# Loading the first 240 tokens of q and k as plain fp32 on two hardware queues, with a new load order, in an attention-plus-MLP kernel

## The chip, the cores and the metric

The kernel runs on one core of one Trainium2 chip. The time is the device time of one execution in microseconds (us). A ratio in this document is the record's comparison of one kernel's fast runs with the fast runs of the kernel before on the same chip; it differs by up to 0.001 from the plain quotient of the two means, and is not the ratio of the medians quoted beside it. A run counts as slow, and is set aside, when it is over 1.5% above the fastest of its kernel; the runs set aside here had a clock of 0.986 to 1.0, so a late load could have made them long as well. Chips differ: the kernel before had a median of 350.9 us on one, 352.4 to 352.9 us on three occasions later.

Words used for the engines: PE is TensorE (PEld its weight loads), DVE is VectorE, ACT is ScalarE, POOL is GpSimd, SP is SyncE. In this kernel each engine runs its instructions in the order in which they were emitted (the 7.82 us wait below shows it for PE). A DMA queue takes its transfers from one engine's order too: q1 is SyncE's queue, q10 is ScalarE's, both fed by hardware; q0 is GpSimd's queue, fed by software, and the only one here whose transfers also convert fp32 to bf16. The profile counts all of them against the same 16 DMA engines.

## The reference, cut to what matters

```python
# q, k, v: [8, 8, 576, 64] fp32; beacon_k, beacon_v: [8, 8, 16, 64] fp32
k_all = concatenate([beacon_k, k], axis=2)            # 592 keys, the first 16 always visible
v_all = concatenate([beacon_v, v], axis=2)
scores = (1 / 8) * q @ k_all^T                        # causal mask on the 576 own keys
a = softmax(scores)
x = (a @ v_all) as [8 * 576, 512]
out = relu(x @ w_in) ** 2 @ w_out                     # 512 -> 2048 -> 512
```

## The kernel before

A list scheduler written in Python orders all operations at build time, with estimated durations. Each engine then executes its fixed list. Batch 0 is split into two parts (its first 240 tokens, then 336) so that the tensor engine can start early; batches 0 and 1 are transposed on the tensor engine, later batches by transposing DMAs. The parts that the change touches:

```python
def add_part_loads(b, part, prio, after, free):      # q/k of batches 0 and 1: GpSimd's queue, cast on the way
    ...
    return [nc.gpsimd.dma_start(out=strided_buf(b, x, part)[:, h],               # bf16
            in_=t[b, h, t0:t0 + np_ * ns, :].rearrange("h (p s) d -> p h s d", s=ns))]

def add_load(b, x, c, prio, behind=[], sync=[]):      # one chunk of 128 rows as fp32, to be cast by an engine
    soft = b in SOFT_V or (b == 0 and c >= 2)         # V chunks 2 to 4 of batch 0: GpSimd's queue
    queue = nc.gpsimd if soft else nc.sync            # V chunks 0 and 1: SyncE's queue
    ...                                               # [128, 8, 64] fp32: pieces of 256 bytes
    engs = ("POOL", "DVE") if b == 0 else ("POOL",)   # who casts it

def add_beacon(b, prio):                              # 32 KB for each of batches 0 and 1
    nc.sync.dma_start(out=bkf[b % 2], in_=beacon_k[b]...)     # bkf is ONE buffer; SyncE's queue
    # DVE casts it, PE transposes it (4 small matmuls), DVE copies it into kT

# order of the first loads on GpSimd's queue:
#   part 0 of q/k, w_in quarter 0, part 1 of q/k, V chunks 2 to 4, w_in quarters 1 to 3, batch 1's q/k, ...
# order of the first loads on SyncE's queue:
#   beacon k 0, beacon v 0, V chunks 0 and 1, beacon k 1, then (after the last w_out load) batch 2 ...
```

The softmax here doesn't subtract the row's maximum and nothing guards it: scores larger than these inputs give would overflow.

## Time and profile before

| | before |
|---|---|
| time, median | 350.9 us |
| span of the profiled run | 348.6 us |
| PE busy | 330.0 us |
| PE idle in the first 15 us | 8.8 us |
| first scores | 9.43 us |
| first AV | 11.32 us |
| transposes of part 1 begin | 14.88 us |

The first fence has lines of the page of the kernel before: the busy time of PE, then the busy tenths of PE and of the DMA engines in 40 equal slices of the span.

```profile
PE 330.0 (95%) x2846; PEld 175.8 (50%) x2884; DVE 171.1 (49%) x394; ACT 191.7 (55%) x290; POOL 92.2 (26%) x139
...
PE   1899999999989979999999999999999999999995
...
DMA  9999979999999999899996999560015011011002
```

PE is the limit nearly everywhere, and the DMA engines are about as busy in the first two thirds. The windows view of the kernel before gives, for each stretch of time, its length, then the busy us and the number of instructions of each engine, the granted clock, the DMA engines' busy share and the GB/s.

```profile
0.00:5.00 5.00, 0.25 (x4) 0.25 (x4) 3.01 (x19) 1.49 (x2) 3.75 (x9) 1.00 0.50 83
5.00:10.00 5.00, 1.71 (x20) 1.00 (x20) 1.75 (x6) 0.66 (x3) 4.99 (x11) 1.00 1.32 162
10.00:15.00 5.00, 4.22 (x52) 2.62 (x54) 4.03 (x17) 3.75 (x7) 4.72 (x6) 1.00 1.44 190
15.00:20.00 5.00, 5.00 (x66) 3.02 (x66) 3.95 (x14) 3.34 (x7) 3.45 (x6) 1.00 1.21 228
20.00:25.00 5.00, 5.00 (x60) 3.42 (x57) 3.07 (x11) 3.50 (x7) 1.95 (x3) 1.00 1.24 207
25.00:30.00 5.00, 5.00 (x75) 3.41 (x73) 4.04 (x16) 4.68 (x9) 1.79 (x2) 1.00 1.30 204
```

The first number behind the comma is PE. In the first 15 us it works 6.18 us and idles 8.82; from then until 60 us it idles only 0.1 us. Those 8.8 us are what the change goes for. The timeline of the kernel before (start, duration, engine, line, operation, count, and in brackets the idle time before it and what ended it) shows the chain of the start:

```profile
4.16 0.32 SPq L380 DMA_DIRECT2D bkf<-in_beacon_k_dram  x1
...
8.13 0.81 PE L443 MATMUL ps<-ident,qk_area 120*64 120x120 bf16 x12 [1.52 <-DMA qk_area<-in_q_dram]
...
8.90 0.58 DVE L292 CAST vb<-stg 128x512 bf16<-128x512 f32 x1
...
9.43 0.49 PE L547 MATMUL strip<-qT,kT 64*128 64x240 bf16 x4 [0.49 <-ACT qT L290]
...
11.32 0.51 PE L595 MATMUL ps<-vb,pt 128*128 128x65 bf16 x6
...
14.88 0.77 PE L443 MATMUL ps<-ident,qk_area 112*64 112x112 bf16 x12
```

PE waits for the casting load of q until 8.13; the scores follow at 9.43 and the first AV at 11.32, for which V chunk 1 was ready early (cast at 8.90).

### The profile page before, as it was taken

What the parts mean: (1) busy time and instruction counts of PE and PEld (TensorE: products, weight loads), DVE (VectorE), ACT (ScalarE), POOL (GpSimd) and SP (SyncE); (2) the same over time, 40 slices, a digit from 0 to 9 for tenths busy, and PEclk for the clock granted to TensorE, in tenths of its full rate; (3) what the DMA queues carried; (4) which work ended last, traced back from release to release, by engine and by line L of the source; (5) the groups of instructions that cost most, each with busy time, mean ns of one, the idle gap of its engine ahead of it and who ended that gap; (6) DMA issues with size and microseconds to landing.
All of it is one profiled execution on the core that took longest, in us unless ns stands there. A gap on an engine that the chain in (4) does not pass through costs nothing.

```text
span 348.6 us, 7192 instructions
## 1 busy us (share of the span) xinstructions
PE 330.0 (95%) x2846; PEld 175.8 (50%) x2884; DVE 171.1 (49%) x394; ACT 191.7 (55%) x290; POOL 92.2 (26%) x139
## 2 busy tenths in 40 slices
PE   1899999999989979999999999999999999999995
PEld 1567775444445435444456775444554444444442
DVE  4778996137656864358544683366423302301300
ACT  1678873267656865457535755478436416615611
POOL 8844804504613804403540453000000000000000
PEclk9999999999999999999999999999999999999999
DMA  9999979999999999899996999560015011011002
GB/s 125 199 203 214 205 131 214 200 215 252 207 186 248 211 217 220 159 161 237 234 202 130 208 232 231 109 190 0 2 60 113 17 60 62 0 60 62 2 26 94
DMA packets 147298, 51.40 MB, mean 147 GB/s; under 512 B 136528, under 2 KB 142160, under 8 KB 147264
## 3 DMA queue, kind: packets, MB, share of 16 engines
q1 hardware_dynamic: 136832, 42.48, 58.4%
q0 software_dynamic: 10432, 8.46, 15.3%
q8 instruction: 22, 0.36, 0.4%
q14 instruction: 12, 0.10, 0.1%
HBM read 37.22 MB, written 9.44 MB: 134 GB/s over the span
## 4 chain that ended last, share of the span: by engine, by line
PE 80%; DMA 12%; SPq 2%; issue 1%; DVE 1%; POOL 1%; ACT 1%; POOLq 0%; ACTq 0%
PE ps L725 32%; PE ps L760 30%; PE ps L595 8%; PE strip L547 7%; DMA kT<-qk_area 5%; SPq L643 2%; PE ps L443 2%; DMA qk_area<-in_q_dram 2%; DMA stg<-in_q_dram 2%; DMA stg<-in_k_dram 1%; DMA stg<-in_v_dram 1%; DMA xT<-xn 1%; PE ps L660 1%; DVE xn L612 0%; POOL qk_area L292 0%
## 5 line engine op out<-in xcount | busy, mean ns | idle before, releaser
L725 PE MATMUL ps<-xT,w_in 128*128 128x512 bf16 (+3 forms) x690 | 134.2, 341 | 1.0 <-DMA xT<-xn 0.3
L760 PE MATMUL ps<-w_out,g 128*128 128x512 bf16 x552 | 130.7, 379 | 1.6 <-issue 0.5
L562 ACT ACTIVATE pt<-strip 128x832 bf16<-128x832 f32 (+4 forms) x128 | 104.1, 863 | 40.9 <-PE strip L547 40.8
L725 PEld LDWEIGHTS <-w_in 128*128 128x128 bf16 x704 | 65.7, 98 | 56.2 <-issue 3.5
L741 ACT ACTIVATE g<-ps 128x512 bf16<-128x512 f32 (+2 forms) x122 | 69.3, 568 | 42.3 <-PE ps L725 40.3
L750 DVE TENSOR_TENSOR g<-g 128x1024 bf16<-128x1024 bf16 (+2 forms) x80 | 51.5, 646 | 73.8 <-ACT g L741 72.4
L760 PEld LDWEIGHTS <-g 128*128 128x128 bf16 x576 | 52.9, 98 | 60.4 <-issue 2.4
L292 POOL CAST qk_area<-stg 128x512 bf16<-128x512 f32 (+2 forms) x60 | 41.8, 705 | 46.3 <-DMA stg<-in_k_dram 31.0
L290 ACT COPY osb<-ps 128x512 f32<-128x512 f32 x24 | 14.1, 586 | 59.1 <-PE ps L760 59.1
L595 PEld LDWEIGHTS <-pt 128*128 128x128 bf16 (+1 forms) x960 | 37.4, 99 | 16.5 <-issue 6.3
L595 PE MATMUL ps<-vb,pt 128*128 128x65 bf16 (+1 forms) x960 | 42.0, 196 | 0.0
L292 POOL CAST vb<-stg 128x512 bf16<-128x512 f32 (+1 forms) x36 | 23.9, 673 | 63.0 <-DMA stg<-in_v_dram 38.3
L547 PE MATMUL strip<-qT,kT 64*128 64x80 bf16 (+7 forms) x400 | 36.8, 288 | 3.9 <-DMA kT<-qk_area 3.1
L612 DVE TENSOR_TENSOR xn<-ps,rcp 128x320 bf16<-128x320 f32 (+2 forms) x72 | 32.7, 454 | 2.6
L611 DVE RECIPROCAL rcp<-ps 128x5 f32<-128x5 f32 (+2 forms) x72 | 13.5, 188 | 32.9 <-PE ps L595 32.7
L572 DVE TENSOR_TENSOR pt<-pt,tri 128x1024 bf16<-128x1024 bf16 (+1 forms) x36 | 24.4, 679 | 10.4 <-ACT pt L562 10.0
L743 DVE TENSOR_SCALAR g<-ps 128x512 bf16<-128x512 f32 (+2 forms) x38 | 22.1, 585 | 13.9 <-PE ps L725 12.8
L547 PEld LDWEIGHTS <-kT 64*128 64x128 bf16 x400 | 12.3, 96 | 22.2 <-issue 12.9
L292 DVE COPY osb<-ps 128x512 f32<-128x512 f32 x12 | 8.3, 692 | 17.5 <-PE ps L760 15.5
L443 PE MATMUL ps<-ident,qk_area 96*64 96x96 bf16 (+2 forms) x176 | 8.5, 251 | 3.4 <-DMA qk_area<-in_k_dram 1.6
L576 DVE TENSOR_TENSOR pt<-pt,tri 80x160 bf16<-80x160 bf16 x32 | 10.7, 333 | 0.0
L290 ACT COPY qT<-ps 128x240 bf16<-128x240 bf16 (+2 forms) x9 | 3.7, 426 | 9.5 <-DVE kT L292 8.4
(33 smaller groups left out, 67.5 us busy)
## 6 DMA issues: line engine op xcount, KB each, us to landing
out_dram<-osb SPq DMA_DIRECT2D x17, 512.0 KB, 3.4
stg<-in_q_dram SPq DMA_DIRECT2D x24, 256.0 KB, 4.9
stg<-in_v_dram SPq DMA_DIRECT2D x19, 256.0 KB, 4.6
stg<-in_k_dram SPq DMA_DIRECT2D x18, 256.0 KB, 5.6
w_in<-in_moe_w_in_dram POOLq DMA_DIRECT2D x4, 512.0 KB, 11.2
w_out<-in_moe_w_out_dram POOLq DMA_DIRECT2D x4, 512.0 KB, 10.4
stg<-in_v_dram SPq DMA_DIRECT2D x7, 224.0 KB, 4.2
stg<-in_k_dram SPq DMA_DIRECT2D x6, 224.0 KB, 3.6
```

What stands on the lines that cost most here:

```text
L290: nc.scalar.copy(dst, src)
L292: eng[e].tensor_copy(dst, src)
L547: nc.tensor.matmul(st[:, hj, at:at + t1 - t0], kT[b % 2][hp, pr, 128 * c:128 * c + 128], qT[b % 2][hp, pr, t0:t1], start=True, stop=True,)
L562: nc.scalar.activation(pt[take_pt.held[2]][:, :, off:off + width], st[:, :, 0:width], AF.Exp, bias=0.0, scale=scale)
L572: nc.vector.tensor_tensor(out=d, in0=d, in1=tri[:, m0:m0 + m, :][:, None].to_broadcast([128, 2, m, 128]), op=ALU.min)
L595: nc.tensor.matmul(a[:, (t - tl[0]) * (D + 1):(t - tl[0] + 1) * (D + 1)], P[0:rr, hj, o:o + 128], vb[b % 2][0:rr, c, h, :], start=(c == 0) ...
L612: nc.vector.tensor_tensor(out=xn[b % 2].rearrange("p t (h d) -> p t h d", d=D)[:, tl[0]:tl[0] + nt, h], in0=a[:, :, 0:D], in1=r[:, :, None ...
L725: nc.tensor.matmul(h[:, lo - spans[0][0]:hi - spans[0][0]], w_in_sb[:, mc, ft * 128:(ft + 1) * 128], xT[:, mc, lo % RING:lo % RING + hi - lo],
L741: nc.scalar.activation(dst, h, AF.Relu, bias=0.0, scale=1.0)
L743: nc.vector.tensor_scalar(out=dst, in0=h, scalar1=0.0, scalar2=None, op0=ALU.max)
L750: nc.vector.tensor_tensor(out=d, in0=d, in1=d, op=ALU.mult)
L760: nc.tensor.matmul(o, G[:, fc, ts * 128:(ts + 1) * 128], w_out_sb[:, fc, :], start=(fc == 0), stop=(fc == NFT - 1))
```

## The change

The intent: get the first q and k without the software queue's delay, and save small work around it. (1) Part 0 of q/k of batch 0 is loaded as plain fp32 by SyncE (k) and ScalarE (q) into the idle output buffers, and cast by VectorE and ScalarE. (2) Two heads of it share a transpose. (3) For batch 0 the AV of both heads goes to one PSUM bank, with one reciprocal and one multiply. (4) The load order is redone: V chunks 2 and 3 of batch 0 move from GpSimd's queue to SyncE's, the first w_in quarter moves behind part 1 of q/k and V chunk 4, the casts of V chunks 2 and 3 may run only on GpSimd, and some estimates of the scheduler change. The core of the diff:

```diff
-        soft = b in SOFT_V or (b == 0 and c >= 2)
+        soft = b in SOFT_V or (b == 0 and c == NT - 1)
         queue = nc.gpsimd if soft else nc.sync
...
-        engs = ("POOL", "DVE") if b == 0 else ("POOL",)
+        engs = ("POOL", "DVE") if b == 0 and c <= 1 else ("POOL",)
...
+    def add_first_loads():
+        raw = [osb[i]... for i in range(2)]                          # fp32
+        for lo, hi in ((0, 1), (1, 2), (2, HP)):                     # head pairs 0; 1; 2 and 3
+            for n, (x, t) in enumerate((("k", k), ("q", q))):
+                    return [(nc.sync, nc.scalar)[n].dma_start(out=raw[n][:, h], in_=t[0, h, ...])]
+                ...
+                strided[0, 0, pr, x] = add(f"fc{x}{pr}", ("DVE", "ACT")[n], ..., emit_cast, ...)
...
-            w_ops["in", i] = add(..., behind=[v_loads[0][4]] if i == 1 else first_loads[0] if i == 0 else [w_ops["in", i - 1]], dma=3.15)
-            if i == 0:
-                first_loads.append(add_part_loads(0, 1, -95.0, [w_ops["in", 0]], []))
+            w_ops["in", i] = add(..., behind=[w_ops["in", i - 1] if i else v_loads[0][4]], dma=3.0)
...
-        for hj in range(2):                                          # one bank and one norm for each head
+        for heads in ([(0, 1)] if b < NSPLIT else [(0,), (1,)]):     # batch 0: both heads at once
```

The scheduler now emits SyncE's first loads as k pair 0, beacon k 0, k pair 1, k pairs 2 and 3, beacon v 0, V chunks 0, 1, 2, 3, and then beacon k 1. Before, beacon k 1 stood behind V chunk 1.

More of the change, by code (lines that the diff above doesn't have):

```diff
@@ L49 @@
     LAT = {"PE": 0.2, "ACT": 0.2, "DVE": 0.15, "POOL": 0.25, "SP": 0.1, "-": 0.0}
+    DMA_LAT = {"SP": 0.6, "ACT": 0.6, "POOL": 2.0}
     def __init__(self, pools, limits):
@@ L80, in run @@
                 release(op)
-        free = {e: 0.0 for e in engines}
+        free = {e: 2.3 if e == "DVE" else 0.0 for e in engines}
         dma_free = 0.0
-        lanes = {"SP": [], "POOL": []}
+        lanes = {"SP": [], "POOL": [], "ACT": []}
         events = [(0.0, 0, None, None)]
@@ L154, in run @@
                     if op.dma:
-                        dma_free = max(dma_free, now + 0.6) + op.dma
+                        dma_free = max(dma_free, now + self.DMA_LAT[e]) + op.dma
                         seen = max(end, dma_free + 1.6)
@@ L235, in strided_buf, with paired @@
         return qk_area[0:np_, at:at + H * ns * D].rearrange("p (h s d) -> p h s d", h=H, s=ns)
+    def paired(x):
+        _, np_, ns = parts_of[0][0]
+        return strided_buf(0, x, 0).rearrange("p (g u) s d -> p (g u s d)", u=2).rearrange(
+            "p (g s e) -> p g s e", g=HP, s=ns)
     bkf = [sb("bkf", [Nb, H, D], FP32)] * 2
@@ L248 @@
     osb = [sb(f"osb{i}", [128, 2, d_model], FP32) for i in range(2)]
-    rcp = [sb(f"rcp{i}", [128, NT], FP32) for i in range(8)]
+    rcp = [sb(f"rcp{i}", [128, 2 * NT], FP32) for i in range(4)]
     tri = sb("tri", [128, 4, 128], BF16)
@@ L265 @@
     nc.vector.memset(warm, 0.0)
-    nc.scalar.activation(warm, warm, AF.Exp)
     for i in range(2):
@@ L270 @@
     for p in pt:
-        for lo, hi in ((928, 1024), (1440, 1536), (1824, 2048)):
-            nc.vector.memset(p[:, :, lo:hi], 0.0)
-    nc.vector.memset(tri, BIG)
+        nc.vector.memset(p[:, :, 928:1952].rearrange("p h (a w) -> p h a w", w=512)[:, :, :, 0:96], 0.0)
+        nc.vector.memset(p[:, :, 1824:2048], 0.0)
     def emit_tri(e):
+        nc.gpsimd.memset(tri, BIG)
         for i in range(4):
@@ L278, in emit_tri @@
                                     base=Nb if i == 0 else 0, pattern=[[1, 128]], channel_multiplier=-1)
-    ident_op = add("ident", "POOL", 0.6, lambda e: make_identity(nc, ident), prio=-199.8)
-    tri_op = add("tri", "POOL", 1.0, emit_tri, prio=-150.0)
+    ident_op = add("ident", "POOL", 1.3, lambda e: make_identity(nc, ident), prio=-300.0)
+    tri_op = add("tri", "POOL", 1.5, emit_tri, prio=-250.0, behind=[ident_op])
     def rows_of(c):
@@ L341, in add_load @@
         ld = add(f"ld{b}{x}{c}", "POOL" if soft else "SP", 1.3 if lo else 0.65, emit_load,
-                 prio=prio, take=("stg", "stg"), dma=1.1 * rows / 128, behind=load_chain[-1:] + behind, sync=sync)
+                 prio=prio, take=("stg", "stg"), dma=1.15 * rows / 128, behind=load_chain[-1:] + behind, sync=sync)
         load_chain.append(ld)
@@ L360, in add_load @@
                 deps += trans[b - 2, x]
-        engs = ("POOL", "DVE") if b == 0 else ("POOL",)
+        engs = ("POOL", "DVE") if b == 0 and c <= 1 else ("POOL",)
         cast[b, x, c] = add(f"cast{b}{x}{c}", engs, {"DVE": 0.6, "POOL": 0.65}, emit_cast,
-                            prio=prio, deps=deps, give=ld)
+                            prio=prio if b else prio - 220.0, deps=deps, give=ld)
     def add_trans(b, x, prio):
@@ L376, in add_trans @@
         deps += [o for p in range(HP * (b - 2), HP * (b - 1)) for o in qk_ops[p]]
-        trans[b, x] = [add(f"tr{b}{x}", "SP", 3.8, emit, prio=prio, deps=deps, dma=3.2)]
+        trans[b, x] = [add(f"tr{b}{x}", "SP", 4.1, emit, prio=prio, deps=deps, dma=3.5)]
     def add_beacon(b, prio):
-        ld = add(f"bkl{b}", "SP", 0.65, lambda e: [nc.sync.dma_start(
+        prio = prio if b else -299.5
+        ld = add(f"bkl{b}", "SP", 0.45, lambda e: [nc.sync.dma_start(
             out=bkf[b % 2], in_=beacon_k[b].transpose([1, 0, 2]))], prio=prio, dma=0.1,
@@ L440, in emit_tp @@
                             for u in range(ns):
+                                at = i * n_tok + u * np_
+                                if b == 0 and part == 0:
+                                    nc.tensor.transpose(pp[:, at:at + np_], paired(x)[:, pr, u], ident[0:np_, 0:np_])
+                                    continue
                                 for hj in range(2):
-                                    at = i * n_tok + u * np_
                                     nc.tensor.transpose(pp[64 * hj:64 * hj + 64, at:at + np_],
                                                         strided_buf(b, x, part)[:, 2 * pr + hj, u, :], ident[0:np_, 0:np_])
-                    tp = add(f"tp{b}.{part}.{pr}{xs}", "PE", 0.75 if b == 0 else 0.6, emit_tp,
+                    tp = add(f"tp{b}.{part}.{pr}{xs}", "PE", 0.1 + (0.1 if b == 0 else 0.075) * ns * len(xs), emit_tp,
                              prio=100.0 * (HP * b + pr) - 190 + 0.1 * n + 1000.0 * part,
@@ L464, in add_strided, with emit, emit_cast, emit_warm @@
                     add(f"tpg{b}.{part}.{pr}{xs}", "-", 0.0, None, deps=evs, give=tp)
+    def add_first_loads():
+        t0, np_, ns = parts_of[0][0]
+        raw = [osb[i].rearrange("p a b -> p (a b)")[0:np_].rearrange("p (h s d) -> p h s d", h=H, s=ns)
+               for i in range(2)]
+        first = []
+        for lo, hi in ((0, 1), (1, 2), (2, HP)):
+            for n, (x, t) in enumerate((("k", k), ("q", q))):
+                h = slice(2 * lo, 2 * hi)
+                def emit(e, t=t, n=n, h=h):
+                    return [(nc.sync, nc.scalar)[n].dma_start(
+                        out=raw[n][:, h],
+                        in_=t[0, h, t0:t0 + np_ * ns, :].rearrange("h (p s) d -> p h s d", s=ns))]
+                o = add(f"fld{x}{lo}", ("SP", "ACT")[n], 0.45, emit, prio=-300.0 + lo + n, dma=0.42 * (hi - lo))
+                first.append(o)
+                for pr in range(lo, hi):
+                    def emit_cast(e, x=x, n=n, pr=pr):
+                        copy_on(e, paired(x)[:, pr].rearrange("p s (u d) -> p u s d", u=2),
+                                raw[n][:, 2 * pr:2 * pr + 2])
+                    strided[0, 0, pr, x] = add(f"fc{x}{pr}", ("DVE", "ACT")[n], (0.33, 0.42)[n], emit_cast,
+                                               prio=-210.0 + pr, deps=[o])
+        def emit_warm(e):
+            nc.scalar.activation(warm, warm, AF.Exp)
+        add("warm", "ACT", 1.5, emit_warm, prio=-290.0, behind=[first[-1]])
     trans_part = {}
@@ L583, in add_phase, with emit_av @@
         norm_ops[p, n] = []
-        for hj in range(2):
-            h = 2 * pr + hj
+        width = nt * (D + 1)
+        for heads in ([(0, 1)] if b < NSPLIT else [(0,), (1,)]):
             box = {}
-            def emit_av(e, hj=hj, h=h, box=box):
+            def emit_av(e, heads=heads, box=box):
                 P = pt[take_pt.held[2]]
                 a = ps[box["av"].held[2]]
-                for t in tl:
-                    for c in range(t + 1):
-                        rr = rows_of(c)
-                        o = ph.off[c, t]
-                        nc.tensor.matmul(
-                            a[:, (t - tl[0]) * (D + 1):(t - tl[0] + 1) * (D + 1)],
-                            P[0:rr, hj, o:o + 128],
-                            vb[b % 2][0:rr, c, h, :],
-                            start=(c == 0), stop=(c == t),
-                        )
-            av = add(f"av{p}.{n}.{hj}", "PE", 0.03 + 0.0325 * sum(t + 1 for t in tl), emit_av, prio=base - 150 + hj,
+                for hj in heads:
+                    at = (hj - heads[0]) * width
+                    for t in tl:
+                        for c in range(t + 1):
+                            rr = rows_of(c)
+                            o = ph.off[c, t]
+                            nc.tensor.matmul(
+                                a[:, at + (t - tl[0]) * (D + 1):at + (t - tl[0] + 1) * (D + 1)],
+                                P[0:rr, hj, o:o + 128],
+                                vb[b % 2][0:rr, c, 2 * pr + hj, :],
+                                start=(c == 0), stop=(c == t),
+                            )
+            nh = len(heads)
+            av = add(f"av{p}.{n}.{heads[0]}", "PE", 0.03 + 0.0325 * nh * sum(t + 1 for t in tl), emit_av,
+                     prio=base - 150 + heads[0],
@@ L603, in add_phase, with emit_norm @@
                      deps=[mask] + [cast[b, "v", c] for c in range(tl[-1] + 1)] + av_ops[p], take=("ps", "av"),
-                     give=take_pt if ph is phases(b)[-1] and hj == 1 else None)
+                     give=take_pt if ph is phases(b)[-1] and heads[-1] == 1 else None)
             box["av"] = av
             av_ops[p].append(av)
-            def emit_norm(e, hj=hj, h=h, box=box):
-                a = ps[box["av"].held[2]][:, 0:nt * (D + 1)].rearrange("p (t d) -> p t d", d=D + 1)
-                r = rcp[(2 * (2 * p + n) + hj) % len(rcp)][:, 0:nt]
-                nc.vector.reciprocal(r, a[:, :, D])
+            def emit_norm(e, heads=heads, nh=nh, box=box):
+                a = ps[box["av"].held[2]][:, 0:nh * width].rearrange("p (h t d) -> p h t d", h=nh, d=D + 1)
+                r = rcp[(2 * (2 * p + n) + heads[0]) % len(rcp)][:, 0:nh * nt].rearrange("p (h t) -> p h t", h=nh)
+                nc.vector.reciprocal(r, a[:, :, :, D])
+                h0 = 2 * pr + heads[0]
@@ L612, in emit_norm @@
                 nc.vector.tensor_tensor(
-                    out=xn[b % 2].rearrange("p t (h d) -> p t h d", d=D)[:, tl[0]:tl[0] + nt, h],
-                    in0=a[:, :, 0:D],
-                    in1=r[:, :, None].to_broadcast([128, nt, D]),
+                    out=xn[b % 2].rearrange("p t (h d) -> p h t d", d=D)[:, h0:h0 + nh, tl[0]:tl[0] + nt],
+                    in0=a[:, :, :, 0:D],
+                    in1=r[:, :, :, None].to_broadcast([128, nh, nt, D]),
                     op=ALU.mult,
@@ L621, in add_phase @@
                 deps += [o for (bb, _), o in xt_ops.items() if bb == b - 2]
-            norm_ops[p, n].append(add(f"norm{p}.{n}.{hj}", "DVE", 0.35 + 0.067 * nt, emit_norm, prio=base - 150 + hj,
-                                      deps=deps, give=av))
+            norm_ops[p, n].append(add(f"norm{p}.{n}.{heads[0]}", "DVE", 0.35 + 0.067 * nt * nh, emit_norm,
+                                      prio=base - 150 + heads[0], deps=deps, give=av))
     xt_ops = {}
@@ L687, in emit @@
                     in_=moe_w_in.rearrange("(m p) f -> p m f", p=128)[:, :, i * w:(i + 1) * w])]
-            w_ops["in", i] = add(f"win{i}", "POOL", 1.3, emit, prio=-100 + i, behind=[v_loads[0][4]] if i == 1 else first_loads[0] if i == 0 else [w_ops["in", i - 1]], dma=3.15)
-            if i == 0:
-                first_loads.append(add_part_loads(0, 1, -95.0, [w_ops["in", 0]], []))
+            w_ops["in", i] = add(f"win{i}", "POOL", 1.3, emit, prio=-100 + i, behind=[w_ops["in", i - 1] if i else v_loads[0][4]], dma=3.0)
     def add_weights_out():
@@ L697, in emit @@
                     in_=moe_w_out.rearrange("(c p) f -> p c f", p=128)[:, i * n:(i + 1) * n, :])]
-            w_ops["out", i] = add(f"wout{i}", "POOL", 1.3, emit, prio=-90 + i, behind=[v_loads[1][4]] if i == 0 else [w_ops["out", i - 1]], dma=3.15)
+            w_ops["out", i] = add(f"wout{i}", "POOL", 1.3, emit, prio=-90 + i, behind=[v_loads[1][4]] if i == 0 else [w_ops["out", i - 1]], dma=3.0)
     def add_chunk(j):
@@ L801 @@
         if b == 0:
-            first_loads = [add_part_loads(0, 0, -200.0, [], [])]
-            add_weights([0])
+            add_first_loads()
+            part_loads = add_part_loads(0, 1, -95.0, [tri_op], [])
         if b < NPE:
@@ L811 @@
             if x == "v" and b == 0:
-                if c == 2:
-                    behind = first_loads[1]
+                if c == NT - 1:
+                    behind = part_loads
             elif x == "v" and b == 1 and c == 0:
@@ L824 @@
         if b == 0:
-            add_weights([1, 2, 3])
+            add_weights(range(4))
         if b == 1:
```

## The prediction

> **What bounds the kernel now.** TensorE: the page gives it 330.0 us busy of a 348.6 us span. The windows view puts 8.8 us of the 18.6 idle us in the first 15 us; from 15 to 60 us only 0.1 us is idle. From 95 to 130 us 3.2 us more are idle, mostly two waits on transposing loads (the timeline: 0.84 us before 101.66, 1.85 us before 128.45, both "DMA kT<-qk_area").
>
> At the start the chain of waits runs over one software-queue q load of 5.77 us, then transposes at 8.13, copies, the first score matmul at 9.43. The first AV runs at 11.32; the transposes of batch 0's second part begin at 14.88.
>
> **What the change does.** (1) The first 240 tokens of q and k come as fp32 on two hardware queues, issued at about 0.8 us without descriptor work on GpSimd. From the trace's small hardware loads (2.1 to 3.0 us to landing) I estimate the first pair at 3.8, casts to 4.3, first scores at 5.5: 4 us earlier. ScalarE's table load (1.28 us), now behind three issues, should just fit before its cast. (2) Two heads share a transpose: 16 fewer, about 76 ns each, but in time that was idle. (3) One reciprocal and multiply for two heads: VectorE is not the limit. (4) The first AV now needs V chunk 1 cast on GpSimd, behind seven DMA issues of about 0.75 us: not before 10.8. V chunks 0 to 3 (1 MB) sit behind 0.98 MB of fp32 q/k, twice the bytes that the casting loads wrote. The Trainium skill, "DMA: Bandwidth & Descriptors", section "Issuing engines are not separate DMA queues", says that all queues end on the same 16 engines, so another queue saves issue time, not bandwidth; the trace's flat 0.2 MB/us from 10 to 47 us agrees. So chunk 1 lands at 10.5-12.5 and the first AV starts at 11-13, no earlier than now, though part 0's scores are done by then.
>
> **How much is critical.** Most of the 4 us is given back at this AV. The second part's transposes start at about 13 instead of 14.9, with 0.8 us of other transposes still owed: 1 to 2.5 us gained by 15 us. Later work is TensorE-bound, so a gain stays if batches 2 to 4 do not stall more. Their loads wait for the last w_out load (the DMA queue's own wait ends at 49.2 us), which bandwidth sets; I expect it within 1 us of now. The changed kernel's instruction order puts 12, 12 and 8 more first-layer matmuls (0.2 us each) before the first scores of batches 2, 3 and 4: about 2.5 us of work fills the waits. Net gain about 2.5 us: 348.7 us, range 345.5 to 351.2. Faster by over 2%: 0.07; within 2%: 0.91; slower: 0.02.
>
> **What would show it.** First scores near 5.5; a TensorE gap of 1 to 4 us before the first AV, ended by GpSimd's V cast; idle in the first 15 us 6 to 8 us; batch 2's first SyncE load still at 49-51; waits on kT at batches 3 and 4 no longer than now; TensorE busy 328-330. The slow clock (240-column matmuls of 214 ns at 21.6, 130 ns from 24.8) should end within 2 us of now.
>
> **What would make it wrong.** V chunk 1 landing at 9 lets the first AV keep more of the 4 us (346). V or second-part loads squeezed to 14-15 us, or w_out 2 us later, eat the gain (351). A clock that warms 3.4 us earlier or later moves 1.5 us.

## The result

The changed kernel gives the right output and takes 361.71 us (four runs, 361.05 to 363.6) against 350.9 us (350.4 to 352.85): slower, ratio 1.0306, 95% interval 1.0249 to 1.0363.

The page of the changed kernel, same lines as before:

```profile
PE 332.1 (92%) x2868; PEld 175.7 (49%) x2868; DVE 170.5 (47%) x374; ACT 194.1 (54%) x294; POOL 89.5 (25%) x137
...
PE   2447899999999998999999799999999999999995
...
DMA  8998999599999999989978999691013111002002
```

PE's work hardly changed (332.1 us; the trace before lacked a few matmul records), but the first four slices are 2, 4, 4 and 7 tenths busy instead of 1, 8, 9 and 9. The windows view of the changed kernel:

```profile
0.00:5.00 5.00, 0.99 (x8) 0.44 (x8) 3.72 (x16) 2.19 (x4) 4.25 (x14) 1.00 0.52 143
5.00:10.00 5.00, 2.21 (x19) 1.26 (x19) 1.76 (x7) 2.40 (x7) 3.08 (x5) 1.00 1.30 211
10.00:15.00 5.00, 1.65 (x14) 0.74 (x13) 1.81 (x5) 2.48 (x4) 0.00 (x0) 1.00 1.32 208
15.00:20.00 5.00, 4.06 (x54) 2.74 (x53) 3.33 (x11) 1.79 (x4) 2.05 (x3) 1.00 1.22 202
20.00:25.00 5.00, 1.82 (x24) 1.04 (x22) 0.41 (x2) 2.08 (x3) 1.24 (x2) 1.00 1.23 202
25.00:30.00 5.00, 0.36 (x6) 0.31 (x8) 0.80 (x3) 0.00 (x0) 1.57 (x3) 1.00 0.67 106
```

PE's first column adds up to 11.09 us of work in 30 us, that is 18.91 us idle; before it was 21.18 us of work and 8.82 idle. The difference, 10.1 us, is most of the 11.8 us between the two profiled spans (348.6 and 360.4 us; the medians are 10.8 us apart). The first 10 us are better than before (3.20 us of work against 1.96). Then PE starves. The timeline of the changed kernel shows on what:

```profile
3.67 7.38 SPq L343 DMA_DIRECT2D stg<-in_v_dram  x4
...
5.48 0.49 PE L586 MATMUL strip<-qT,kT 64*128 64x240 bf16 x4 [0.48 <-ACT qT L296]
...
11.17 7.09 SPq L387 DMA_DIRECT2D bkf<-in_beacon_k_dram  x1
11.36 0.43 DVE L298 CAST vb<-stg 128x512 bf16<-128x512 f32 x1 [1.93 <-DMA stg<-in_v_dram]
...
12.15 0.49 PE L586 MATMUL strip<-qT,kT 64*128 64x240 bf16 x4 [1.70 <-DVE kT L298]
...
15.21 0.61 POOL L298 CAST vb<-stg 128x512 bf16<-128x512 f32 x1 [7.13 <-DMA stg<-in_v_dram]
...
15.87 0.71 PE L636 MATMUL ps<-vb,pt 128*128 128x65 bf16 x10 [2.30 <-POOL vb L298]
...
28.43 0.62 POOL L298 CAST vb<-stg 128x512 bf16<-128x512 f32 x1 [5.33 <-DMA stg<-in_v_dram]
...
29.64 0.27 PE L398 MATMUL ps<-ident,bks 16*128 16x16 bf16 x4 [7.82 <-DVE bks L390]
```

The first scores start at 5.48 us, as hoped. Then PE waits 1.70 us, until 12.15, for a copy of keys that stands in VectorE's order behind the cast of V chunk 0, which itself waited 1.93 us for its load. V chunk 1 is cast at 15.21 (8.90 before), and PE waits 2.30 us for it. Then PE stands still for 7.82 us, from 21.82 to 29.64, in front of four tiny matmuls: the transposes of batch 1's beacon keys, which nothing needs before batch 1's scores, much later. They stand there in PE's fixed order, and their 32 KB load has not landed. The chain that ended last in the changed kernel, its first 30 us (start, us, what), says the same:

```profile
4.03 7.14 DMA stg<-in_v_dram
11.17 17.97 DMA bkf<-in_beacon_k_dram
```

That load took 18 us from issue to landing; the issue alone took SyncE 7.09 us where it took 0.32 us before. It sat behind 1 MB of V in SyncE's queue. V itself crawled: V chunk 3 was cast at 28.43 us. Why V crawled, the DMA view of 14 to 18 us of the changed kernel shows: queue, its packets, MB and share of time.

```profile
q0 software_dynamic: 625, 0.63, 91.2%
q1 hardware_dynamic: 626, 0.16, 29.7%
```

The two queues moved the same number of packets, but q0's are 1 KB rows of w_in (0.63 MB / 625) and q1's are 256-byte rows of V. So SyncE's queue got 0.16 of 0.79 MB, one fifth of the bytes. The even count holds from 12 to 18 us. From 8 to 10 us, beside part 1's q/k loads, it is 493 (q0) to 910. The DMA views of 22 to 24, 24 to 26 and 26 to 28 us count 342 to 185, 393 to 126 and 303 to 49 packets, although V chunk 3 and the beacon had not landed; what held their last packets back is not shown. The Trainium skill, "DMA: Bandwidth & Descriptors", section "Queues, rings and completion order", says that each DMA engine takes turns between queues at packet granularity. This trace agrees, if a packet is what the profile counts as one.

### The profile page after: what moved, and what is told of

Same layout as the page of the kernel before. It is cut to its first block, busy times and chain, and to the rows that moved or that the text cites. A ratio compares the mean times of both kernels' runs of the same rounds, so it can differ in the third digit from the quotient of the medians.

```text
span 360.4 us, 7180 instructions
## 1 busy us (share of the span) xinstructions
PE 332.1 (92%) x2868; PEld 175.7 (49%) x2868; DVE 170.5 (47%) x374; ACT 194.1 (54%) x294; POOL 89.5 (25%) x137
## 3 DMA queue, kind: packets, MB, share of 16 engines
q0 software_dynamic: 8160, 7.44, 12.5%
## 4 chain that ended last, share of the span: by engine, by line
PE 76%; DMA 16%; SPq 3%; DVE 2%; POOL 1%; issue 1%; ACT 0%; POOLq 0%; DVEq 0%; ACTq 0%
PE ps L802 32%; PE ps L767 30%; PE ps L636 7%; PE strip L586 6%; DMA bkf<-in_beacon_k_dram 5%; DMA stg<-in_v_dram 4%; DMA kT<-qk_area 3%; DMA stg<-in_q_dram 1%; DMA stg<-in_k_dram 1%; SPq L343 1%; PE ps L453 1%; SPq L375 1%; DMA osb<-in_q_dram 1%; PE ps L704 1%; POOL vb L298 0%
## 5 line engine op out<-in xcount | busy, mean ns | idle before, releaser
L802 PE MATMUL ps<-w_out,g 128*128 128x512 bf16 x576 | 134.8, 379 | 0.0
L792 DVE TENSOR_TENSOR g<-g 128x1024 bf16<-128x1024 bf16 (+2 forms) x80 | 52.5, 660 | 71.9 <-ACT g L783 70.8
L298 POOL CAST vb<-stg 128x512 bf16<-128x512 f32 (+1 forms) x39 | 26.6, 690 | 86.5 <-DMA stg<-in_v_dram 71.2
L296 ACT COPY osb<-ps 128x512 f32<-128x512 f32 x29 | 17.0, 585 | 57.4 <-PE ps L802 56.1
L636 PEld LDWEIGHTS <-pt 128*128 128x128 bf16 (+1 forms) x960 | 37.5, 99 | 18.4 <-issue 7.1
L656 DVE TENSOR_TENSOR xn<-ps,rcp 128x320 bf16<-128x320 f32 (+2 forms) x64 | 31.5, 491 | 2.7 <-DVE rcp L654 0.4
L654 DVE RECIPROCAL rcp<-ps 128x5 f32<-128x5 f32 (+2 forms) x64 | 12.3, 192 | 42.6 <-PE ps L636 42.4
L615 DVE TENSOR_TENSOR pt<-pt,tri 80x160 bf16<-80x160 bf16 x32 | 12.1, 377 | 0.0
L298 DVE COPY osb<-ps 128x512 f32<-128x512 f32 x7 | 4.8, 692 | 11.4 <-PE ps L802 11.1
L450 PE MATMUL ps<-ident,qk_area 120*128 120x120 bf16 x16 | 2.5, 299 | 5.9 <-DVE qk_area L298 5.9
## 6 DMA issues: line engine op xcount, KB each, us to landing
w_in<-in_moe_w_in_dram POOLq DMA_DIRECT2D x4, 512.0 KB, 11.8
```

What stands on the lines that cost most here:

```text
L296: nc.scalar.copy(dst, src)
L298: eng[e].tensor_copy(dst, src)
L636: nc.tensor.matmul(a[:, at + (t - tl[0]) * (D + 1):at + (t - tl[0] + 1) * (D + 1)], P[0:rr, hj, o:o + 128], vb[b % 2][0:rr, c, 2 * pr + hj ...
L656: nc.vector.tensor_tensor(out=xn[b % 2].rearrange("p t (h d) -> p h t d", d=D)[:, h0:h0 + nh, tl[0]:tl[0] + nt], in0=a[:, :, :, 0:D], in1= ...
L792: nc.vector.tensor_tensor(out=d, in0=d, in1=d, op=ALU.mult)
L802: nc.tensor.matmul(o, G[:, fc, ts * 128:(ts + 1) * 128], w_out_sb[:, fc, :], start=(fc == 0), stop=(fc == NFT - 1))
```

## The experiments

Rival theories of the 7.8 us wait, and of the loss. **A**: the placing of one small load behind V in an in-order queue is the whole cause. **B**: all of SyncE's plain loads starve, because the queues take turns by packet and w_in has packets four times as large; the beacon is only the first victim that PE meets. A third one: the fp32 load's doubled bytes simply delay everything. Three of the first four kernels were made from the changed kernel by moving emitted operations after the scheduler had run, and the fourth, w_in_narrow, by splitting loads in place, so that every engine order not mentioned is identical.

"Idle" is PE's idle time in the first 30 us of the profiled run, 30 us minus the PE column of the windows view. "AV" is when the first AV matmul that needs V chunk 1 ran. Medians are of the fast runs; two of four runs of v23_cast_queue, one of four of w_in_narrow and two of six of v_casts_dve were set aside as slow. With these runs the plain quotients of the means are 1.003, 1.009 and 1.007.

| kernel | median us | ratio, 95% interval | idle | AV |
|---|---|---|---|---|
| before | 350.9 to 352.9 | 1 | 8.8 | 11.3 |
| changed | 361.71 | 1.0306 (1.0249 to 1.0363) | 18.9 | 15.9 |
| bk1_early | 357.54 | 1.0147 (1.0109 to 1.0185) | 13.6 | 18.4 |
| v23_cast_queue | 351.41 | 0.9978 (0.9921 to 1.0035) | 10.2 | 15.0 |
| v23_again | 353.54 | 1.004 (1.000 to 1.008) | 11.7 | 16.5 |
| casts_before_w_in | 356.09 | 1.0113 (1.0056 to 1.017) | 11.9 | 16.8 |
| w_in_narrow | 354.64 | 1.0068 (1.0011 to 1.0126) | 12.3 | 14.3 |
| av_only | 353.28 | 1.0013 (0.998 to 1.0045) | 9.5 | – |
| v_casts_dve | 354.51 | 1.0042 (0.9986 to 1.0098) | slow run | slow run |
| v23_hold | 352.73 | 1.0005 (0.9966 to 1.0044) | 9.7 | 14.4 |
| v_casts_dve_hold | 352.23 | 0.9977 (0.9943 to 1.0011) | 7.4 | 11.8 |
| hold_again | 352.68 | 1.0018 (0.9976 to 1.0059) | 7.1 | 11.5 |

### bk1_early

```diff
+    # bkf for batch 1 is a view of the still unused g[1] instead of the shared buffer
+    # order of emission: beacon k 1 directly behind beacon k 0
```

> The changed kernel with one move: batch 1's beacon-k load (32 KB) is issued second on the SyncE queue, into a buffer of its own, instead of behind the four V loads; every other engine's order is the same. Theory A (a small load stuck behind 1 MB of V in one queue stalls TensorE through its in-order transposes): if that placement alone is the cause, the 7.8 us TensorE wait at 21.8 goes and the time falls by 7 to 8 us, to about 354. Theory B (all plain loads on the SyncE queue starve while the casting queue is busy; V chunks 2 and 3 land just as late): TensorE waits instead for the GpSimd casts of V chunks 3 and 4, which end at 29 to 31 us, and only about 1 us comes back: 360 to 361.

Measured: 357.54 us, ratio 1.0147, half of the loss back. The beacon landed 4.1 us after its issue and the 7.8 us wait was gone. It is between the two forecasts, and the trace says why. V chunk 1 was slower still (cast at 17.75 us, and PE waited 4.19 us for it). As GpSimd stood at that cast, it issued the third and fourth w_in loads at 18.31 us instead of 15.76, which left SyncE's queue to itself for a while: V chunk 3 was cast at 22.66 instead of 28.43 and chunk 4 at 24.55 instead of 30.48, in time for PE. So A's placement cost about half, and B's sum was wrong because it kept the old times of V chunks 3 and 4.

### v23_cast_queue

```diff
-        queue = nc.gpsimd if soft else nc.sync
+        queue = nc.gpsimd if soft or (b == 0 and x == "v" and c >= 2) else nc.sync
+    # order of emission: V chunks 2 and 3 behind part 1's last q load on GpSimd, as before the change
```

> The changed kernel with V chunks 2 and 3 of batch 0 moved back to the GpSimd queue, behind the second-part q/k loads and ahead of V chunk 4; every other order is the same. Both theories A and B: batch 1's beacon load lands before 16 us, V chunks 2 and 3 are cast before 22 us, no TensorE wait over 2 us after 16 us; time 349 to 353. If only the doubled bytes of the fp32 q/k load were to blame, little would change: 358 or more.

Measured: 350.39, 352.43, 355.66 and 355.77 us; the last two were set aside as slow, and the ratio of the other two is 0.9978. With the second run (v23_again, below) the fair reading is "within half a per cent of the kernel before". The interval of that second measurement reaches 0.8%. The wait for the beacon was gone, though its load landed at about 16.9 us, after the 16 us forecast, and after 15.03 us no wait before 100 us reached 0.3 us. So moving two V loads of 256 KB each to SyncE's queue is what cost the 3%. The fp32 q/k load is still in this kernel, so its doubled bytes are not the main cause.

### casts_before_w_in

```diff
+    # order of emission on GpSimd: the casts of V chunks 1, 2, 3 directly behind V chunk 4's load,
+    # so ahead of all four w_in loads
```

> The changed kernel with one move on GpSimd: the casts of V chunks 1, 2 and 3 stand ahead of the four w_in loads, so that no w_in load is issued before these chunks have landed. The V and beacon loads stay on the SyncE queue, and all bytes are the same. Theory B (packet turns against the w_in loads starve the SyncE queue): V chunk 3 lands at about 13 us instead of 28, the beacon at about 14 instead of 29, the 7.8 us wait goes, the first w_in load lands at about 18; time 349 to 353. If the SyncE queue is slow by itself or by total bytes, V chunk 3 lands after 20 us and the time stays over 357.

Measured: 356.09 us, ratio 1.0113; 4 of 10.8 us remain lost instead of nothing. (The forecast was 349 to 353 us.) In 14 to 18 us SyncE's queue now moved twice as much. The DMA view of that stretch in this kernel:

```profile
q1 hardware_dynamic: 1255, 0.31, 41.8%
q0 software_dynamic: 22, 0.02, 1.9%
```

So the queue is not slow by itself: V chunk 3 and the beacon starved because of w_in. V chunk 1 gained nothing. With no w_in load issued before 18.20 us, its cast on GpSimd still waited for its load until 16.09 us (15.21 in the changed kernel):

```profile
16.09 1.28 POOL L303 CAST vb<-stg 128x512 bf16<-128x512 f32 x2 [9.52 <-DMA stg<-in_v_dram]
```

What held V chunk 1 up is found further below, in v23_hold. V chunk 3 was cast at 17.64 us, 10.8 us earlier than in the changed kernel, though not at the 13 us forecast, because part 1's q/k loads and V chunk 4, which this kernel did not hold back, took their turns until about 14 us. PE did not wait for the beacon. The price stands in the windows view of this kernel:

```profile
15.00:20.00 5.00, 3.17 (x48) 2.44 (x47) 2.45 (x8) 1.07 (x4) 3.59 (x6) 1.00 0.21 35
```

The last number is 35 GB/s: with w_in held back until 18.2 us the DMA engines ran dry, and everything behind came later. Batch 2's first load, which waits for the last w_out load, was issued at 54.19 us instead of 49.70 before.

### w_in_narrow

```diff
-                    out=w_in_sb[:, :, i * w:(i + 1) * w], ...)]
+                    out=w_in_sb[:, :, a:a + w // 2], ...)
+                    for a in (i * w, i * w + w // 2)]
```

> The changed kernel with each w_in load split into two of half the columns: destination packets of 512 bytes instead of 1 KB, the same bytes and order. If engines take turns by packet, the counts of packets of the two queues stay about equal while both have work (312 and 311 in 14 to 16 us in the changed kernel), so the SyncE queue's share of the bytes rises from about 1/5 to 1/3, and V chunk 3 and the beacon land some 4 to 6 us earlier (beacon at 23 to 25 us); time 355 to 358. If the share is by bytes or the casting queue has priority, the beacon still lands at about 29 and the time stays at 361 to 362.

Measured: a median of 355.48 us over all four runs (352.79 to 358.62) and 354.64 over the three fast ones, ratio 1.0068. The profiled run was the fastest, 352.79 us. The DMA view of 14 to 18 us in this kernel:

```profile
q0 software_dynamic: 981, 0.49, 88.3%
q1 hardware_dynamic: 978, 0.25, 46.6%
```

Packets are equal again (981 and 978), and with w_in's packets halved the bytes are now 2 to 1 instead of 4 to 1. The beacon's cast started at 22.57 us instead of 29.16, and PE waited 2.81 us for it instead of 7.82:

```profile
23.08 0.27 PE L398 MATMUL ps<-ident,bks 16*128 16x16 bf16 x4 [2.81 <-DVE bks L390]
```

The counts and shares forecast for turns by packet held. The casts of V chunk 3 and of the beacon came 6.3 and 6.6 us earlier, a little more than the 4 to 6 us forecast, and the median of the fast runs is just below the 355 to 358 us named. The split also doubles the number of w_in issues on GpSimd: the first half of w_in took 3.08 us to issue instead of 1.53, and this may account for part of the gain in time, but not for the equal packet counts. A share by bytes, or a right of way for q0, would have left the bytes at 4 to 1. Theory B's mechanism is shown for 14 to 18 us; A names the place where it hurts.

### av_only

The kernel before with part (3) of the change alone, rescheduled.

> The kernel before with one part of the change alone: the AV of both heads of batch 0 in one bank, with one reciprocal and one multiply for two heads; loads as before. Both theories: VectorE and the banks are not what TensorE waits for, so nothing moves: ratio 0.995 to 1.005. If the one-bank AV were part of the loss, over 1.005.

Measured: ratio 1.0013, interval 0.998 to 1.0045. The one-bank AV is neutral.

### v23_again, v_casts_dve, v23_hold, v_casts_dve_hold, hold_again: where the hoped-for gain went

With the V loads back in their old queue, the change still gains nothing. In v23_cast_queue the first AV with V chunk 1 runs at 15.03 us, later than before (11.32), so the early scores are wasted. Two further edits, apart and together:

```diff
 # v_casts_dve: v23_cast_queue, and
+    # order of emission: casts of V chunks 0 and 1 on DVE, behind the key copy of pair 3
 # v23_hold: v23_cast_queue, and;  v_casts_dve_hold: v_casts_dve, and
+                if op.name == "sld0k1.0":        # first load of part 1 on GpSimd
+                    wait_for(its DMA, the load of k pair 1)
```

> The kernel v23_cast_queue with the casts of V chunks 0 and 1 on VectorE behind the key copies of pair 3, instead of one on VectorE ahead of them and one on GpSimd. Theory: V chunk 1 is late because its transfer is (14.3 us, in turns with the second-part q/k loads), not because of the casting engine: the first AV on chunk 1 still starts at 13.5 to 15 us and the time stays within 0.5% of v23_cast_queue's ratio 0.998. If the place of the cast were the cause, the first AV would start by 12 us and 2 us come back.

Measured: ratio 1.0042; its six runs spread from 351.54 to 357.54 us. The profiled run was slow, so its trace is not used here and the forecast of the AV's start is neither confirmed nor refuted. The ratio is 0.6% above v23_cast_queue's 0.998, not within the 0.5% forecast. The time did not fall by 2 us.

> v23_cast_queue again, unchanged, because its four runs spread over 5.4 us (350.39 to 355.77) and two of them were set aside as slow though their clock was full. If the spread belongs to the kernel (V chunk 1 still lands late, at a time set by the turns between queues), this chip shows it too: runs from 350 to 356, mean 0 to 0.5% above the kernel before. If it was the other chip, all runs lie within 3 us and the ratio is 0.995 to 1.000.

Measured: 351.45 to 355.65 us, ratio 1.004, AV at 16.48 us in this profile (a 354.67 us run) against 15.03 in the earlier one (a 350.39 us run). The spread showed on the second chip too, as it should if it belongs to the kernel.

> v23_cast_queue with the hold of the second-part loads alone; the casts of V chunks 0 and 1 stay where the changed kernel has them, chunk 1 on GpSimd behind the second w_in load. Theory: chunk 1 now lands at about 10 us but its cast stands behind nine DMA issues that start 3 us later, so the first AV on it starts at 13.5 to 14.5 us: about 1 us better than v23_cast_queue at the start, ratio 0.998 to 1.003. If the hold alone were enough, the AV starts by 12 us and the ratio is that of v_casts_dve_hold.

Measured: AV at 14.39 us, ratio 1.0005; as expected, the hold alone is not enough, since the cast stands behind the DMA issues. But the hold shows what made V chunk 1 late: it landed 5.6 us after its issue, against 10.2 us in v23_cast_queue and 11.5 in v23_again. In v23_cast_queue it shared the DMA engines with part 1's q/k loads, and with what follows them on GpSimd's queue, which the hold delays too.

> The kernel v_casts_dve with the four second-part q/k loads held on GpSimd until the second fp32 k load has landed (about 6 us instead of 2.9 us), so that V chunks 0 and 1 do not share the DMA engines with them. Theory: V chunk 1 lands at 9 to 10.5 us, the first AV on it starts at 10 to 11 us, the second part's transposes at 12.5 to 13.5 us, TensorE idle in the first 15 us falls from 10 to 7 us or less; 2 to 3 us faster than v_casts_dve and 1 to 3 us faster than the kernel before (ratio 0.991 to 0.998). If V chunk 1 is late for another reason, the first AV stays at 13 us or later and the second part's loads only get later: ratio 1.000 or more.

Measured: AV at 11.77 us (10 to 11 was forecast), 7.44 us idle in the first 15 us (7 or less was forecast), no PE wait of 0.3 us between 11.34 us and batch 3's first scores at 102.16 us, ratio 0.9977.

> v_casts_dve_hold again, unchanged, beside the two others on one chip. Theory: first AV at 11.5 to 12 us again, runs within 3 us of each other, ratio 0.994 to 1.000, the fastest of the three. If the first result was luck, the ratio is over 1.000.

Measured: AV at 11.46 us, runs 350.43 to 354.73 us, ratio 1.0018, level with v23_hold. The AV came as forecast; the runs spread over 4.3 us instead of 3, the kernel was not the fastest of the three, and by the forecast's own test (a ratio over 1.000) the 0.9977 of the first measurement was luck. The windows view of hold_again:

```profile
0.00:5.00 5.00, 0.92 (x8) 0.45 (x8) 3.05 (x16) 2.30 (x4) 2.19 (x11) 1.00 0.56 143
5.00:10.00 5.00, 2.48 (x22) 1.46 (x20) 2.50 (x8) 2.70 (x7) 3.96 (x6) 1.00 1.37 217
10.00:15.00 5.00, 4.45 (x60) 2.97 (x58) 4.43 (x13) 3.40 (x7) 4.67 (x6) 1.00 1.29 214
```

PE idles 7.15 us in the first 15 us, 1.7 us less than before. That is a real gain at the start, repeated on a second chip, and yet the two measurements of this kernel average a ratio of 1.000. It may be given back later. PE's waits from 40 us on, of hold_again:

```profile
PE strip L595 <- DMA kT<-qk_area: 5.4, 3, 2.1
```

and of the kernel before (total us, times, longest):

```profile
PE strip L547 <- DMA kT<-qk_area: 3.1, 3, 1.9
```

Batches 2 to 7 get their keys by a chain of SyncE loads, GpSimd casts and transposing DMAs that starts when the last w_out load has landed, and so should depend on the bytes moved, not on when PE began. That start hardly moved (first batch-2 load at 49.73 us in hold_again and 48.78 in v_casts_dve_hold, against 49.70). A PE that is ready earlier would wait for the same keys longer: 2.3 us more, against 1.7 us won. This balance is a reading, not shown. In av_only the same view gives 4.9 us, with loads as before and no gain at the start, so 2.3 us is within what profiles differ by. And PE's idle time over the whole span is 17.2 us in hold_again against 18.6 before; what is longer is its busy time, 334.0 us against 330.0, with a mean granted clock of 0.995 in that run against 1.0 and with some matmul records missing before. The profiles come from different chips, and no experiment here shortened that chain. Where the 1.7 us went stays open; it is hardly larger than the uncertainty of a ratio (0.4%, or 1.4 us). No version measured beats the kernel before by more than its noise.

## Why the prediction was wrong

- **Right: the early start.** First scores at 5.48 us (forecast 5.5). ScalarE's table load did fit before its cast. The one-bank AV is neutral, as said (av_only 1.0013); two heads for one transpose was not tested alone.
- **Wrong, mis-sized: "chunk 1 lands at 10.5-12.5 and the first AV starts at 11-13".** Its cast waited for the transfer until 15.21 us, and the AV ran at 15.87; part 1's transposes followed at 16.51 instead of the 13 forecast. The prediction's sum has the 0.98 MB ahead of V in its queue and a total of 0.2 MB/us; it does not name part 1's q/k loads, which ran beside V on GpSimd's queue. With these held back until about 6 us, chunk 1 landed 5.6 us after its issue instead of 10.2 (v23_hold against v23_cast_queue); with w_in held back instead it came no earlier (casts_before_w_in). The prediction had named V at 14 to 15 us as a risk, priced at 351 us.
- **Wrong, by omission: the wait that cost most.** No step of the prediction followed batch 1's beacon load. In the changed order of SyncE it stands behind V chunks 2 and 3, and PE's order has its transposes at about 21 us. It landed at 29.1 us; PE waited 7.82 us. The prediction's passage from the Trainium skill, that another queue saves issue time and not bandwidth, was read as if the choice of queue did not matter to a load's landing; for V chunks 2 and 3 and the beacon behind them it did, because SyncE's packets of V are a quarter of w_in's and took even turns with them (625 to 626). The orders of both engines were there to be read before the run. The prediction checked what the first scores and the first AV wait for, and stopped there.
- **Wrong: "1 to 2.5 us gained by 15 us".** PE idled 10.15 us in the first 15 us against 8.82.
- **Wrong: "w_out within 1 us of now".** Batch 2's first load was issued at 52.95 us instead of 49.70. GpSimd, which issues w_in and w_out, stood in order at casts of V (7.13 and 5.33 us of waits are in the fence above), and from 25 to 30 us the DMA engines moved only 106 GB/s against 204. The prediction had named "w_out 2 us later" as a risk, but priced it at 351 us.
- **Wrong: the clock.** PE runs the same matmul slower early in the kernel (the slow clock) than later. Before, eight 240-column matmuls took 1.78 us at 21.58 us (222 ns each) and four took 0.57 us at 24.80 us; in the changed kernel the first four of their kind took 0.58 us at 33.63 us (145 ns each). The fast clock is first seen about 9 us later, not within 2 us.
- **Partly right: more work in front of batches 2 to 4 fills the waits for kT.** In the changed kernel these waits did not vanish (3.8 us against 3.1). Once the start was repaired they came to 5.4 us in one profile, but to 2.0 and 3.1 us in the two of v23_cast_queue; whether a gain of 2.5 us would have been lost there was not tested.

## What to carry to other kernels

Before moving a load to another queue, list what stands behind it in that queue and what each engine's fixed order waits for next; a 32 KB load behind 1 MB stops the tensor engine as surely as a large one. From 14 to 18 us here, bytes went in proportion to packet size (0.16 to 0.63 MB), so a load in 256-byte rows starved beside one in 1 KB rows: put urgent small-row loads in front of it, or in the same queue. A gain at the start of a kernel may be lost at the next shared limit, here perhaps the DMA chain behind the weights, which did not start earlier.

## What the Trainium skill lacked or had wrong

- "DMA: Bandwidth & Descriptors", section "Queues, rings and completion order": turns at packet granularity are borne out in 14 to 18 us (625 to 626 packets; 981 to 978 with narrower w_in), but the page does not draw the consequence that bytes follow packet size: 0.63 to 0.16 MB, and 0.49 to 0.25 MB. Its packets of several descriptors can't be told apart here; what took even turns is what the profile counts as packets.
- The same page, section "Issuing engines are not separate DMA queues": it says that issuing from several engines only saves sequencer time. The total rate did stay near 0.2 MB/us, but the queue in which a load stands moved its landing: the same 32 KB took 18.0 us behind V and 4.1 us ahead of it, and two V loads in the other queue are worth about 3% of the kernel.
- "Perfetto Trace Analysis", section "DMA Instruction — HWDGE (DVE, Sync)": it shows the issue window to hold the generation of descriptors, with a buffer that can fill, but gives no size. Here the issue of the same 32 KB load took 0.32 us in the free queue and 7.09 us behind four V loads, so a long SyncE issue was a sign of a backed-up queue in these runs.
